# Opening two output tiles at once in the first chunk of an attention-plus-MLP kernel, with narrower filler matmuls in its prologue

## The chip, the cores and the metric

The kernel runs on one core of one Trainium2 chip. The metric is the device time of one execution in microseconds (us). A core has a matrix engine (TensorE, PE in the profile; PEld is its weight load), a vector engine (VectorE, DVE), a scalar engine (ScalarE, ACT), GpSimd (POOL) and a queue engine (SyncE, SP), each with its own queue of instructions, and 16 DMA engines that they share.

## The reference

```python
B, H, S, D = 8, 8, 576, 64            # q, k, v; s is (B, H, S)
scores = q @ k.T / sqrt(D)
cum = cumsum(maximum(s, 0), -1)
bias = -(cum[..., :, None] - cum[..., None, :])
scores = where(causal, -1e9, scores + minimum(bias, 0))
attn = softmax(scores) @ v            # per batch and head
x = attn as (B * S, H * D)            # 4608 tokens x 512
h = x @ w_in                          # 512 -> 2048
out = gelu_exact(h) @ w_out           # 2048 -> 512
```

## The kernel before

The tokens are worked on in nine chunks of 512 (NCH = 9), the attention in eight batches of eight heads, taken as four pairs of heads (p = 0 to 3). The order of all work is written out by hand; each engine runs its instructions in the order of the program, and the framework adds the waits. While the MLP of chunk c runs, the attention of batch c + 1 is placed between its pieces.

The pieces, with their lines:

- `tr_item(b, p, i)` (353) transposes one pair's q (i = 0) or k (i = 1) on PE with 18 small matmuls, and a copy, mostly on DVE (364), puts the result into `qkT`. Only batches 0 and 1 are transposed so.
- `sc_item(b, p)` (370) makes the scores of a pair in two units, u = 0 and 1 (376), in two-bank tiles. ACT takes the exponential into P (392), and DVE applies the causal mask (401, 406). In the prologue the mask is partly added on PE (384).
- `av_item(b, p)` (452) multiplies P with v and with the weights (414), and `norm` (427) divides by way of a logarithm and an exponential on ACT (431, 432) and a product on DVE (447), which fills `xT`, the input of the MLP. `av_rest` and `norm_rest` do the last 64 tokens of a batch.
- `l1_item(c, f2)` (482) is the MLP's first layer, for two blocks of 128 columns of w_in (495), with the Gelu on ACT (501, 504) into `gT`.
- `l2_item(c, sub, f0, f1, av)` (506) is the second layer for 128 tokens: one output tile `o_ps` of 128 x 512 is the sum of 16 matmuls (514), ft = 0 to 15; f0 and f1 say which of the 16 this call issues. The call that ends at 16 also issues the copy of the tile on DVE (521) and the output's DMA on SP (523). ft = 0 to 7 read the first half of w_out, 8 to 15 the second.
- `scale_pair(b, p)` (550) scales one pair's part of v on DVE (230).
- `keep_busy(n)` (559) issues n filler matmuls of 512 columns on a zero tile, into `warm`; nothing reads it.

On-chip accumulation memory (PSUM) has eight banks of 128 x 512 fp32. Four are the two "sc" tiles (scores, first layer, wide attention outputs), three are "av" (transposes, attention outputs, some output tiles), one is "mlp" (an output tile, or `warm`). With `av=False` an output tile takes the "mlp" bank, with `av=True` one of the three "av" banks. A tile takes its bank at its first matmul and gives it back after its last reader.

Loads go through POOL's queue in the order of the program: q and k of batch 0, v of batch 0, w_in in four parts (`load_w(0, i)`), then the first halves of q and k of batch 1, w_out in four parts (`load_w(1, i)`), the second halves of q and k, v of batch 1, and q and k of batch 2.

The change touches the prologue, from line 563 on, in which filler matmuls stand between the transposes and scores of batch 0, and the branch `c == 0` of the loop over chunks, lines 630 to 676. There, once chunk 0's first layer is done, its four output tiles (sub = 0 to 3) are computed between the transposes, scores and attention outputs of batch 1.

Of the kernel before, what the change touches and what calls it, by code (L numbers as in the profile page):

```python
# [19 lines left out]
def kernel(  # L20
# [10 lines left out]
    nc = tc.nc  # L31
# [92 lines left out]
    busy = const.tile([128, 512], bf16, name="busy")  # L124
# [245 lines left out]
    def sc_item(b, p, neg=False, masks=True):  # L370
        P_of[b, p] = P = work.tile([128, 2, PW], bf16, tag="P", bufs=4, name="P")
        for u in range(NU):
            s_ps = ps.tile([128, 2, 512], fp32, tag="sc", bufs=2, name="sc_ps")
            for jt, i0, n, off in UNITS[u]:
                for e in range(2):
                    nc.tensor.matmul(  # L376
                        s_ps[:, e, off : off + n],
                        lhsT=qkT[b % 2][e * 64 : e * 64 + 64, 1, p, jt * 128 : jt * 128 + 128],
                        rhs=qkT[b % 2][e * 64 : e * 64 + 64, 0, p, i0 : i0 + n],
                        start=True, stop=not neg, skip_group_check=neg,  # L380
                    )
            for lo, n, w in ((0, 2, 128), (448, 1, 64))[: u + 1 if neg else 0]:
                for e in range(2):
                    nc.tensor.matmul(  # L384
                        s_ps[:, e, 0:512].rearrange("p (g c) -> p g c", c=256)[:, :, 0:128]
                        if n == 2 else s_ps[:, e, lo : lo + w],
                        lhsT=ident_bf,
                        rhs=neg_bf[:, :w].unsqueeze(1).to_broadcast([128, n, w])
                        if n == 2 else neg_bf[:, :w],
                        start=False, stop=True, skip_group_check=True,  # L390
                    )
            nc.scalar.activation(  # L392
                P[:, :, UO[u] : UO[u] + UW[u]], s_ps[:, :, : UW[u]], func=AF.Exp, scale=scale
            )
            if masks and not neg:
                mask_item(b, p, u, nc.vector)
# [109 lines left out]
    def l2_item(c, sub, f0=0, f1=FT, av=False):  # L506

        gT = gT_of[c]
        if f0 == 0:
            tag, bufs = ("av", 3) if av else ("mlp", 1)  # L510
            o_of[c, sub] = ps.tile([128, KO * 128], fp32, tag=tag, bufs=bufs, name="o_ps")
        o_ps = o_of[c, sub]
        for ft in range(f0, f1):
            nc.tensor.matmul(  # L514
                o_ps, lhsT=gT[:, ft, sub * 128 : (sub + 1) * 128], rhs=w_out_r[:, ft, :],
                start=(ft == 0), stop=(ft == FT - 1),
            )
        if f1 < FT:
            return
        o_sb = work.tile([128, KO * 128], fp32, tag="osb", bufs=3, name="o_sb")  # L520
        nc.vector.tensor_copy(o_sb, o_ps)  # L521
        r0 = c * NB + sub * 128
        nc.sync.dma_start(out=out[r0 : r0 + 128, :], in_=o_sb)
# [32 lines left out]
    load_v(0, (ST - 1,))  # L556
    warm = ps.tile([128, 512], fp32, tag="mlp", bufs=1, name="warm")

    def keep_busy(n):
        for _ in range(n):  # L560
            nc.tensor.matmul(warm, lhsT=busy[:, :128], rhs=busy, start=True, stop=True)

    weights_scan()
    keep_busy(8)
    tr_item(0, 0, 0, nc.scalar.copy)
    tr_item(0, 0, 1)
    weights_dve()
    keep_busy(3)
    sc_item(0, 0, masks=False)
    tr_item(0, 1, 0)  # L570
    keep_busy(1)
    tr_item(0, 1, 1)
    nc.vector.tensor_scalar(neg_bf, tri_bf, 2048.0, -2048.0, op0=MULT, op1=ALU.add)
    weights_pe()
# [31 lines left out]
    for c in range(NCH):  # L606
        nb = c + 1
        for k0, k1 in ((0, 2), (2, 3)) if c == 0 else ((0, 3),):
            l1_item(c, 0, k0, k1)
            l1_item(c, 1, k0, k1)  # L610
        l1_item(c, 0, KO - 1)
        l1_item(c, 1, KO - 1)
        l1_item(c, 2, av=True)
        if 0 < c and nb < B:
            scale_v(nb, STS, nc.vector)
            absmax_v(nb)
        if c == 0:
            absmax_v(0)
            scale_v(0, STS[ST - 1 :], nc.vector)
        if c < B:  # L620
            for p in range(NP):
                absmax(c, p)
        if 1 < c and nb + 1 < B:
            nc.gpsimd.tensor_copy(pace, gT_of[c][:, 0, 0:1])
            load_v(nb + 1)
            if nb + 2 < B:
                load_qk(nb + 2)
        for f2 in range(3, FT // 2):
            l1_item(c, f2)
        if c == 0:  # L630
            exp_set()
            load_v(2)
            for p in range(NP):
                av_rest(0, p)
            tr_item(1, 0, 0)
            tr_item(1, 0, 1)
            l2_item(c, 0, 0, 8)
            tr_item(1, 1, 0)
            tr_item(1, 1, 1)
            norm_rest(0)  # L640
            sc_item(1, 0)
            l2_item(c, 0, 8)
            sc_item(1, 1)
            l2_item(c, 1, 0, 8, av=True)
            tr_item(1, 2, 0)
            tr_item(1, 2, 1)
            l2_item(c, 1, 8, av=True)
            tr_item(1, 3, 0)
            tr_item(1, 3, 1)
            scale_pair(1, 0)  # L650
            sc_item(1, 2)
            l2_item(c, 2, 0, 8)
            scale_pair(1, 1)
            sc_item(1, 3)
            l2_item(c, 2, 8)
            scale_pair(1, 2)
            av_item(1, 0, rest=False)
            scale_pair(1, 3)
            av_item(1, 1, wide=True, rest=False)
            l2_item(c, 3, 0, 8)  # L660
            interleave(2, "q")
            write_rows(2, 0, nc.sync)
            av_item(1, 2, wide=True, rest=False)
            l2_item(c, 3, 8)
            interleave(2, "k")
            write_rows(2, 1, nc.sync)
            av_item(1, 3, rest=False)
            for p in (0, 1):
                transpose_rows(2, p)
            gelu_set()  # L670
            for p in (2, 3):
                transpose_rows(2, p)
            nc.gpsimd.tensor_copy(pace, qkT[0][:, 1, 3, 0:1])
            load_qk(3)
            load_v(3)
            absmax_v(1)
        elif nb < B:
            exp_set()
            l2_item(c, 0, 0, 4)
            if c == 1:  # L680
                for p in range(NP):
                    av_rest(1, p)
            sc_item(nb, 0)
            if c == 1:
                norm_rest(1)
            l2_item(c, 0, 4)
            late = int(c == 1)
            for p in range(1, NP):
                if nb + 1 < B and p == 1 + late:
                    interleave(nb + 1, "q")  # L690
                    write_rows(nb + 1, 0, nc.sync)
                if nb + 1 < B and p > 1 and not late:
                    transpose_rows(nb + 1, p - 2)
                sc_item(nb, p)
                av_item(nb, p - 1)
                l2_item(c, p, 0, 12)
                if p == NP - 1:
                    if nb + 1 < B:
                        for pt in range(0 if late else p - 1, NP):
                            transpose_rows(nb + 1, pt)  # L700
                    if c == 1:
                        nc.gpsimd.tensor_copy(pace, qkT[(nb + 1) % 2][:, 1, p, 0:1])
                        load_qk(nb + 2)
                    av_item(nb, p)
                    norm_rest(nb)
                    gelu_set()
                l2_item(c, p, 12)
                if nb == B - 1 and p == 1:
                    cert_decay()
                if nb + 1 < B and p == 1 + late:  # L710
                    interleave(nb + 1, "k")
                    write_rows(nb + 1, 1, nc.sync)
        else:
            if c == B - 1:
                cert_1()
            for sub in range(4):
                if c == NCH - 1 and sub == 3:
                    l2_last(c, sub)
                    break
                l2_item(c, sub, av=sub % 2 == 0)  # L720
                if c == B - 1 and sub < 3:
                    (cert_2, cert_3, cert_4)[sub]()
# [4 lines left out]
    with tc.If(rv > 0):  # L727
        with tc.tile_pool(name="gen", bufs=1) as gen, tc.tile_pool(
# [21 lines left out]
            with tc.For_i(0, B, 1) as b:  # L750
# [8 lines left out]
                for h in range(H):  # L759
# [17 lines left out]
                    for it in range(ST):  # L777
                        n_i = 128 if it < ST - 1 else SL
                        w = min(S, (it + 1) * 128)
                        s_ps = gps.tile([128, 1024], fp32, tag="g2", bufs=2, name="gs_ps")  # L780
                        for j0 in range(0, w, 512):
# [3 lines left out]
                                rhs=tT["k"][:, j0:j1], start=True, stop=True,  # L785
# [20 lines left out]
                        for jt in range(it + 1):  # L806
# [9 lines left out]
                                lhsT=raw["v"][:n_j, jt, h0 : h0 + 2, :].rearrange("p h d -> p (h d)"),  # L816
                                rhs=pT[:n_j, :n_i], start=(jt == 0), stop=(jt == it),
# [5 lines left out]
            with tc.For_i(0, NCH, 1) as c:  # L823
                g = gen.tile([128, FT, NB], bf16, name="gg")
                for ft in range(FT):
                    h_ps = gps.tile([128, NB], fp32, tag="g4", bufs=1, name="gh_ps")
                    for ko in range(KO):
                        nc.tensor.matmul(
                            h_ps, lhsT=w_in_r[:, ko, ft * 128 : (ft + 1) * 128],
# [44 lines left out]
```

## Time and profile before

| | us |
|---|---|
| median of six runs | 331.74 |
| lowest and highest of the six | 330.57 and 333.61 |
| the profiled execution | 332.1 |
| its span, first to last instruction | 330.2 |
| PE busy in the span | 317.6 |
| ACT busy | 203.1 |
| DVE busy | 192.8 |
| POOL busy | 65.4 |
| start of the steady first layer of chunk 0 (495) | 23.09 |
| first output tile's first matmul | 38.13 |

The profile is of one execution, and times in it count from its first instruction. A timeline row gives the start, the duration, the engine, the line, the operation, the tile written and those read, the shapes, how many instructions are merged in the row, and in brackets how long the engine stood idle before it and what ended that. A matmul's duration in such a row includes the time in which it drains; starts of successive matmuls tell what one costs. A few matmul records are missing from the trace, so a count can be one short.

### The profile page before, as it was taken

What the parts mean: (1) busy time and instruction counts of PE and PEld (TensorE: products, weight loads), DVE (VectorE), ACT (ScalarE), POOL (GpSimd) and SP (SyncE); (2) the same over time, 40 slices, a digit from 0 to 9 for tenths busy, and PEclk for the clock granted to TensorE, in tenths of its full rate; (3) what the DMA queues carried; (4) which work ended last, traced back from release to release, by engine and by line L of the source; (5) the groups of instructions that cost most, each with busy time, mean ns of one, the idle gap of its engine ahead of it and who ended that gap; (6) DMA issues with size and microseconds to landing.
All of it is one profiled execution on the core that took longest, in us unless ns stands there. A gap on an engine that the chain in (4) does not pass through costs nothing.

```text
span 330.2 us, 6357 instructions
## 1 busy us (share of the span) xinstructions
PE 317.6 (96%) x2540; PEld 164.2 (50%) x2585; DVE 192.8 (58%) x384; ACT 203.1 (62%) x288; POOL 65.4 (20%) x100
## 2 busy tenths in 40 slices
PE   6989999999999999999999999999999999999992
PEld 2654555445554555445544554455445544444452
DVE  5749378896569364946395748755783664150021
ACT  4697657759566857677577757677659566204400
POOL 8753243005300730610043003200000000000000
PEclk9699999999999999999999999999999999999998
DMA  7999999855985899999669665527500110010012
GB/s 116 221 210 204 206 185 241 284 93 88 242 266 107 149 250 275 208 131 232 218 133 232 177 177 126 138 105 172 137 3 34 52 48 0 34 64 32 3 64 71
DMA packets 53828, 47.30 MB, mean 143 GB/s; under 512 B 31328, under 2 KB 43872, under 8 KB 53792
## 3 DMA queue, kind: packets, MB, share of 16 engines
q0 software_dynamic: 15936, 23.07, 39.7%
q1 hardware_dynamic: 37856, 23.75, 26.3%
q8 instruction: 22, 0.36, 0.5%
q14 instruction: 14, 0.11, 0.1%
HBM read 36.85 MB, written 16.52 MB: 162 GB/s over the span
## 4 chain that ended last, share of the span: by engine, by line
PE 92%; DMA 2%; DVE 1%; issue 1%; ACT 1%; POOL 1%; POOLq 0%
PE h_ps L495 37%; PE o_ps L514 37%; PE sc_ps L376 5%; PE avn L414 4%; PE avd L414 3%; DMA early_k<-in_k_dram 2%; PE avr L414 1%; PE tr_ps L359 1%; PE o_ps L533 1%; PE avw L414 1%; PE sc_ps L384 0%; DVE qkT L364 0%; POOL early_q L115 0%; ACT ln L432 0%; ACT ln L431 0%
## 5 line engine op out<-in xcount | busy, mean ns | idle before, releaser
L514 PE MATMUL o_ps<-w_out_r,gT 128*128 128x512 bf16 x533 | 127.3, 380 | 1.7 <-issue 0.5
L495 PE MATMUL h_ps<-xT,w_in_r 128*128 128x512 bf16 x560 | 125.2, 379 | 1.5 <-DVE xT L447 0.6
L495 PEld LDWEIGHTS <-w_in_r 128*128 128x128 bf16 x576 | 56.2, 98 | 68.6 <-issue 1.1
L501 ACT ACTIVATE gT<-h_ps 128x1024 bf16<-128x1024 f32 x54 | 54.3, 1022 | 49.4 <-PE h_ps L495 49.4
L392 ACT ACTIVATE P<-sc_ps 128x1024 bf16<-128x1024 f32 x64 | 62.2, 1021 | 33.5 <-PE sc_ps L376 31.1
L514 PEld LDWEIGHTS <-gT 128*128 128x128 bf16 x560 | 51.6, 98 | 59.0
L521 DVE COPY o_sb<-o_ps 128x512 f32<-128x512 f32 x35 | 24.1, 687 | 46.4 <-PE o_ps L514 46.4
L401 DVE TENSOR_TENSOR P<-P,tri_bf 128x512 bf16<-128x512 bf16 x58 | 23.9, 422 | 36.8 <-ACT P L392 36.4
L213 DVE TENSOR_REDUCE amx<-qkT 128x2 f32<-128x1152 bf16 x32 | 40.9, 1336 | 0.0
L447 DVE SCALAR_TENSOR_TENSOR xT<-avn,ln 128x256 bf16<-128x256 f32 (+3 forms) x64 | 21.7, 386 | 24.9 <-ACT ln L432 24.8
L202 POOL DMA_DIRECT2D raw_v<-in_v_dram x40 | 34.2, 880 | 9.9 <-DMA w_out_r<-in_moe_w_out_dram 4.1
L431 ACT ACTIVATE ln<-avd 128x256 f32<-128x256 f32 x56 | 18.6, 392 | 12.4 <-PE avd L414 11.0
L230 DVE TENSOR_TENSOR vv<-raw_v,wb 128x512 bf16<-128x512 f32 (+3 forms) x44 | 25.2, 634 | 0.8 <-DMA raw_v<-in_v_dram 0.8
L432 ACT ACTIVATE ln<-ln 128x512 f32<-128x512 f32 (+1 forms) x40 | 23.5, 587 | 1.3
L504 ACT ACTIVATE gT<-h_ps 128x512 bf16<-128x512 f32 x36 | 19.6, 603 | 6.3 <-PE h_ps L495 6.3
L220 DVE TENSOR_REDUCE amv<-raw_v 128x1 f32<-128x2048 f32 (+1 forms) x16 | 23.0, 1471 | 0.0
L376 PE MATMUL sc_ps<-qkT 64*128 64x256 bf16 (+2 forms) x320 | 21.9, 258 | 0.5 <-DVE vv L230 0.4
L376 PEld LDWEIGHTS <-qkT 64*128 64x128 bf16 x320 | 13.2, 96 | 14.8 <-issue 12.4
L414 PEld LDWEIGHTS <-vv 128*64 128x64 bf16 x384 | 16.9, 109 | 6.9 <-issue 4.1
L414 PEld LDWEIGHTS <-wb 128*64 128x64 bf16 x384 | 17.1, 111 | 0.0
L414 PE MATMUL avn<-P,vv 128*64 128x256 bf16 x224 | 16.1, 265 | 0.0
L414 PE MATMUL avd<-P,wb 128*64 128x256 bf16 x224 | 15.4, 259 | 0.0
(94 smaller groups left out, 158.5 us busy)
## 6 DMA issues: line engine op xcount, KB each, us to landing
out_dram<-o_sb SPq DMA_DIRECT2D x35, 256.0 KB, 2.3
raw_v<-in_v_dram POOLq DMA_DIRECT2D x32, 256.0 KB, 8.0
rows<-qk_bf SPq DMA_DIRECT2D x12, 576.0 KB, 6.1
early_q<-in_q_dram POOLq DMA_DIRECT2D x14, 288.0 KB, 10.7
early_k<-in_k_dram POOLq DMA_DIRECT2D x14, 288.0 KB, 11.4
w_in_r<-in_moe_w_in_dram POOLq DMA_DIRECT2D x4, 512.0 KB, 11.1
w_out_r<-in_moe_w_out_dram POOLq DMA_DIRECT2D x4, 512.0 KB, 15.7
raw_v<-in_v_dram POOLq DMA_DIRECT2D x8, 128.0 KB, 9.7
```

What stands on the lines that cost most here:

```text
L202: nc.gpsimd.dma_start(out=t[:n_st, st, :, :], in_=bass.AP(tensor=v.tensor, offset=v.offset + b * H * S * D + st * 128 * D, ap=[[D, n_st], ...
L213: nc.vector.tensor_reduce(amx[:, b * NP + p], qkT[b % 2][:, :, p, :S], axis=AX, op=ALU.max, apply_absolute_value=True)
L230: eng.tensor_tensor(vb[:n_st, st0:st1, h0:h1, :], t[:n_st, st0:st1, h0:h1, :], wb[:n_st, st0:st1, b * H + h0 : b * H + h1] .unsqueeze(3).t ...
L376: nc.tensor.matmul(s_ps[:, e, off : off + n], lhsT=qkT[b % 2][e * 64 : e * 64 + 64, 1, p, jt * 128 : jt * 128 + 128], rhs=qkT[b % 2][e * 6 ...
L392: nc.scalar.activation(P[:, :, UO[u] : UO[u] + UW[u]], s_ps[:, :, : UW[u]], func=AF.Exp, scale=scale)
L401: eng.tensor_tensor(d, d, tri_bf.unsqueeze(1).unsqueeze(1).to_broadcast([128, 2, 2, 128]), op=MULT)
L414: nc.tensor.matmul(out[e * 64 : e * 64 + 64, lo : lo + n], lhsT=(wb[:, jt, b * H + h : b * H + h + 1].to_broadcast([128, 64]) if den else ...
L432: nc.scalar.activation(ln[:, :w], ln[:, :w], func=AF.Exp, scale=-1.0)
L495: nc.tensor.matmul(h_of[c, f2][i], lhsT=w_in_r[:, ko, ft * 128 : (ft + 1) * 128], rhs=xT[:, ko, c * NB % XW : c * NB % XW + NB], start=(ko ...
L501: nc.scalar.activation(gT_of[c][:, f2 * 2 : f2 * 2 + 2, :], hh_of[c, f2], func=AF.Gelu)
L514: nc.tensor.matmul(o_ps, lhsT=gT[:, ft, sub * 128 : (sub + 1) * 128], rhs=w_out_r[:, ft, :], start=(ft == 0), stop=(ft == FT - 1),)
L521: nc.vector.tensor_copy(o_sb, o_ps)
```

## The change

In the prologue `keep_busy` gets a width: the three fillers ahead of the first scores and the one ahead of the second pair's k become 256 columns wide in place of 512. The eight at the start and the one ahead of the last scores stay at 512.

In chunk 0 the first half of the second output tile (sub = 1) is issued ahead of the second half of the first (sub = 0), so that both are open at once, the first in the "mlp" bank and the second in an "av" bank. The third tile (sub = 2) goes into an "av" bank in place of the "mlp" bank.

```diff
-    def keep_busy(n):
+    def keep_busy(n, w=512):
         for _ in range(n):
-            nc.tensor.matmul(warm, lhsT=busy[:, :128], rhs=busy, start=True, stop=True)
+            nc.tensor.matmul(warm[:, :w], lhsT=busy[:, :128], rhs=busy[:, :w], start=True, stop=True)
...
     weights_dve()
-    keep_busy(3)
+    keep_busy(3, 256)
     sc_item(0, 0, masks=False)
     tr_item(0, 1, 0)
-    keep_busy(1)
+    keep_busy(1, 256)
     tr_item(0, 1, 1)
...
             sc_item(1, 0)
+            l2_item(c, 1, 0, 8, av=True)
+            sc_item(1, 1)
             l2_item(c, 0, 8)
-            sc_item(1, 1)
-            l2_item(c, 1, 0, 8, av=True)
             tr_item(1, 2, 0)
             tr_item(1, 2, 1)
             l2_item(c, 1, 8, av=True)
...
             sc_item(1, 2)
-            l2_item(c, 2, 0, 8)
+            l2_item(c, 2, 0, 8, av=True)
             scale_pair(1, 1)
             sc_item(1, 3)
-            l2_item(c, 2, 8)
+            l2_item(c, 2, 8, av=True)
```

## The prediction

> **What bounds the kernel now.** I read the page first: busy time by engine, then the slices.
>
> ```profile
> span 330.2 us, 6357 instructions
> PE 317.6 (96%) x2540; PEld 164.2 (50%) x2585; DVE 192.8 (58%) x384; ACT 203.1 (62%) x288; POOL 65.4 (20%) x100
> PEclk9699999999999999999999999999999999999998
> ```
>
> TensorE (PE) is busy for 96% of the span. The change touches two stretches, the prologue (to 23 us) and the second half of chunk 0 (41 to 55 us). The clock row shows one dent, in the second slice. The windows view, cut at the edges of that dent and one step before and after it, columns PE, PEld, DVE, ACT, POOL busy, then granted clock, DMA share and GB/s:
>
> ```profile
> 4.16:7.57 3.41, 2.69 (x51) 1.34 (x49) 2.69 (x4) 1.03 (x2) 3.41 (x7) 1.00 1.07 147
> 7.57:10.98 3.41, 2.41 (x65) 1.76 (x66) 2.19 (x4) 2.03 (x4) 3.41 (x5) 1.00 1.12 217
> 10.98:14.40 3.42, 3.42 (x70) 2.45 (x70) 1.64 (x5) 2.69 (x3) 3.03 (x6) 0.50 1.04 225
> 14.40:17.81 3.41, 3.05 (x22) 1.28 (x25) 3.37 (x8) 2.20 (x3) 0.52 (x4) 0.50 1.20 204
> 17.81:21.22 3.41, 3.12 (x60) 2.87 (x58) 0.14 (x1) 3.25 (x7) 2.38 (x5) 1.00 1.25 209
> ```
>
> PE runs at half clock from 10.98 to 17.81 us, after two stretches in which it was busy 2.69 and 2.41 of 3.41 us; and DMA is saturated throughout. Then the timelines of the stretch of chunk 0: PE first, then VectorE (DVE), then the POOL queue, which issues the loads.
>
> ```profile
> 40.65 0.61 PE L376 MATMUL sc_ps<-qkT 64*128 64x256 bf16 x10
> 41.20 1.90 PE L514 MATMUL o_ps<-w_out_r,gT 128*128 128x512 bf16 x7
> 43.03 0.61 PE L376 MATMUL sc_ps<-qkT 64*128 64x256 bf16 x10
> 43.57 1.90 PE L514 MATMUL o_ps<-w_out_r,gT 128*128 128x512 bf16 x8
> ```
>
> ```profile
> 40.48 1.42 DVE L364 COPY qkT<-tr_ps 128x576 bf16<-128x576 bf16 x2 [1.10 <-PE tr_ps L359]
> ...
> 43.53 0.68 DVE L521 COPY o_sb<-o_ps 128x512 f32<-128x512 f32 x1
> ...
> 45.92 1.42 DVE L364 COPY qkT<-tr_ps 128x576 bf16<-128x576 bf16 x2
> 48.03 0.69 DVE L521 COPY o_sb<-o_ps 128x512 f32<-128x512 f32 x1 [0.69 <-PE o_ps L514]
> ```
>
> ```profile
> 42.24 0.63 POOL L101 DMA_DIRECT2D early_q<-in_q_dram  x1 [2.92 <-DMA w_out_r<-in_moe_w_out_dram]
> ...
> 45.49 0.61 POOL L101 DMA_DIRECT2D early_q<-in_q_dram  x1 [0.66 <-DMA early_k<-in_k_dram]
> ```
>
> The reader is to see that no PE row names a wait: from 36.8 to 60.5 us PE is busy 23.16 of 23.64 us, and what is missing is the step from one kind of matmul to the next. The bound there is PE's own work. The two POOL rows show how near the loads are: POOL stood on the last quarter of w_out until just before 42.24, and on the second half of batch 1's k until just before 45.49. By the tile view the one was issued at 24.14 and took 17.8 us, landing at 41.96; the other was issued at 27.91 and took 17.3, landing at 45.20.
>
> **What the Trainium skill says.** "TensorE: Matmul & The Clock Gate", section "What's actually happening": the clock is set to half or full by how busy PE was in free-running windows of 3413 ns. The trace agrees in length: the half-clock stretch is 6.83 us, two such windows. The threshold isn't given, and the trace shows only that 2.69 and 2.41 us were together too little. Same page, "Architectural detail": VectorE is a strict FIFO; the trace agrees, no DVE row starts before the one ahead of it. "PSUM — Partial Sum Buffer", "PSUM bank collisions raise a hardware error": order accesses by bank. So a tile in a reused bank waits for the last reader of that bank; two open tiles in two banks do not disturb each other.
>
> **The change, part by part.** No instruction is added or removed, apart from the width of four fillers.
>
> (1) *Fillers.* Four of 512 columns become 256. Three starts at full clock lie 0.216 to 0.225 us apart (timeline at 5.82, 6.05 and 6.26 us), so half the width removes about 0.11 us each, 0.43 us in all, of PE work. None of it is on the path: the three end near 6.5 to 6.6, and the scores behind them start at 6.75, when DVE's copy into qkT (5.93 + 0.76 = 6.69) is done. The fourth starts at about 8.75 and ends before 9.03, when the transposes behind it start on k from DMA (idle before them 0.30, released by early_k). Direct worth: 0.0. Cover gone: had the loads come earlier, at most 0.11 + 0.32 us. The indirect cost is that the first stretch above falls from 2.69 to about 2.37 us busy, and the second from 2.41 to 2.30. If the clock then drops one window sooner (7.57), PE's work from 9.03 to 10.98, continuous, is done at half speed: 0.98 us lost. If it also returns one window later (21.22), another 3.12 / 2 = 1.56. A gain is bounded below in the rivals. Value taken: 0, since the dent came without the change and the same dent stays likeliest.
>
> (2) *Second tile's first half ahead of the first tile's second half.* Both are eight matmuls of 0.216 us (1.83 us with the step), so PE's order is shifted by nothing: scores at 43.03, transposes at 45.40 as before. What moves is the needs. The last quarter of w_out, landed at 41.96, was read at 41.20 + 4 x 0.216 = 42.07, a margin of 0.11 us; now it is read at 43.57 + 0.86 = 44.44, a margin of 2.5. In this execution that removes no wait. The next load behind it is k at 45.20, read at 45.71: margin 0.5. So where PE arrives earlier, the gain is the difference of these margins, at most 0.4 us, before k stops it.
> The second tile now takes its bank at 41.20. The three banks of the attention outputs are handed out in the order they came free (the program's addresses of before), so it gets that of the first transpose of pair 1, whose copy starts at 40.48 and takes 0.75: free at 41.23, plus the 0.05 that lies between qkT's copy and the scores at 6.75. Cost: at most 0.1 us, all on PE. Were it the bank of the batch's leftovers (DVE 41.81 + 0.42 = 42.23), it would cost 1.1; that is the upper end, against which the address order speaks.
>
> (3) *DVE's queue.* The first tile's copy (0.68) and its output DMA on SP's queue move from 43.53 to behind the masks of the second scores, which end at 45.99. Queued behind it: the two transposes' copies, 45.92 to 47.34, now 46.67 to about 48.09, and the second tile's copy behind these, from 48.03 to about 48.1. PE's next transposes at 47.92 and 48.23 reuse those two banks, free at about 47.4 and 48.1: margins 0.5 and 0.1. The scores at 48.61 need the second copy: margin 0.5. Cost 0, and 0.1 to 0.2 if DVE runs late. The pieces of v behind it wait for DMA until 50.82 in any case; that hides the shift. SP holds nothing else until 58.69, so the output DMA delays nothing.
>
> (4) *Third tile in an attention bank.* It starts at 49.15 in the bank that the second tile's copy leaves at about 48.8: margin 0.35, cost 0. The first attention pair at 53.36 takes the two others, empty since 50.1. The fourth tile at 55.02 no longer waits for the third's copy (54.05 + 0.68 = 54.73): a margin of 0.29 becomes several us, worth nothing while it was not late.
>
> **Sum.** For the profiled execution, span 330.2 and 332.1 us with what lies around it: 0 (fillers) + 0.1 (bank) + 0 + 0 = 332.2. In executions whose PE is earlier, up to -0.4. That one execution lies 0.4 above the median of the six runs, 331.74, which themselves go from 330.57 to 333.61. I carry the difference over, between +0.1 and -0.4, as about 0: **331.7**.
>
> **Rivals.** *Slower, through the clock.* The thinner fillers leave the window from 4.16 to 7.57 under the threshold. For it: PE's 2.69 us there is already close to the 2.41 after which the clock fell, and 0.32 goes away. Against it: fillers at 1.20 to 4.55 are unchanged, and the fall came a whole window after the idle gap, so two windows may count. Price: 0.98 for one window, 2.54 for two, thus 332.7 to 334.3; it passes 0.5% (1.66 us) from the point where the clock also comes back later. I name 334.0. Chance 0.2.
> *Faster, through the clock and the loads.* If the dent starts a window earlier and ends one earlier, 14.40 to 17.81 is run at full clock: 3.05 / 2 = 1.5 gained, 0.98 lost. But k at 45.20 caps what arrives, at 0.5 us in this execution; over 0.5% needs the loads earlier as well, which tracing may well delay. Time 330.0. Chance 0.1.
> *It doesn't do what it says*, two tiles opened together relieve no wait, since PE showed none: this is the forecast itself, with the small signs above. Chance 0.7.
>
> **How the numbers follow.** The 0.7 has its own range, 330.6 to 332.8: -0.4 to +0.2, plus the scatter of a median drawn from runs that lie 3.0 us apart, about 0.8 either way. The range for 8 in 10 reaches into the slower rival for one window, and a little to the faster: 330.2 to 333.4. About 0.5% is what a measurement of this kernel can tell from no change. Faster by more: 0.09; within: 0.71; slower by more: 0.20, the two-window case and a late bank together.
>
> **What would show it.** Right: the o_ps rows at about 41.3 and 43.6 with transposes at 45.4 or 45.5; no wait on w_out or on DVE above 0.1 us; the clock dent still two windows of 3.41 us. Step 1 is wrong if the dent begins one window earlier or lasts three. Step 2 is wrong if PE stands over 0.1 us ahead of the second tile on DVE, or if w_out had held PE in the runs that were not traced. Step 3 is wrong if transposes or scores after 47.9 us wait on DVE's copies. A median outside 330.2 to 333.4 would say that an effect in the prologue, and not the order of the tiles, decides.

## The result and the profile after

The changed kernel takes 333.05 us (median; 329.81 to 334.92) against 331.62 for the kernel before in the same comparison: ratio **1.0030**, 95% interval 1.0015 to 1.0044. It is slower by about 1.0 us. The medians lie 1.4 us apart, since the times fall into groups and a median jumps between them; the means, 332.88 and 331.88, differ by 1.00, as the ratio does. Executions that were disturbed as a whole are left out of the ratios, the means and the counts below. The time lies in the predicted range, 330.2 to 333.4, and within the 0.5% that the text calls no change, but the forecast said 331.7 and none, and the interval excludes none.

The profiled execution took 332.84 us. First the head of its page (busy time by engine, then the granted clock in 40 slices):

```profile
span 331.1 us, 6358 instructions
PE 318.9 (96%) x2541; PEld 165.0 (50%) x2585; DVE 193.3 (58%) x384; ACT 203.1 (61%) x288; POOL 65.5 (20%) x100
PEclk9589999999999999999999999999999999999998
```

The dent in the clock is deeper. The windows view of the same execution, cut at its own changes of clock (columns as before: PE, PEld, DVE, ACT, POOL busy, clock, DMA share, GB/s):

```profile
5.05:8.46 3.41, 2.16 (x64) 1.54 (x60) 1.93 (x3) 1.20 (x2) 3.41 (x6) 1.00 1.11 163
8.46:11.87 3.41, 3.41 (x52) 2.07 (x52) 2.38 (x4) 1.86 (x4) 3.41 (x6) 0.50 1.15 245
11.87:15.29 3.42, 3.42 (x70) 2.39 (x69) 1.60 (x5) 2.69 (x3) 2.64 (x6) 0.50 1.06 209
15.29:18.70 3.41, 3.05 (x24) 1.31 (x23) 3.24 (x7) 2.33 (x3) 0.18 (x1) 0.50 1.24 207
18.70:22.11 3.41, 3.18 (x62) 2.93 (x58) 0.27 (x1) 3.25 (x7) 3.39 (x5) 1.00 1.24 208
```

Here the clock fell at the end of the first window at full clock, in which PE was busy 2.16 us, and stayed at half for three windows, 10.24 us; before it had fallen after the second and stayed for two. Chunk 0's first layer starts its unbroken run at 23.85 us in place of 23.09.

The stretch of chunk 0, PE, then DVE:

```profile
41.41 0.61 PE L376 MATMUL sc_ps<-qkT 64*128 64x256 bf16 x10
42.05 1.89 PE L514 MATMUL o_ps<-w_out_r,gT 128*128 128x512 bf16 x7
43.87 0.61 PE L376 MATMUL sc_ps<-qkT 64*128 64x256 bf16 x10
44.41 1.90 PE L514 MATMUL o_ps<-w_out_r,gT 128*128 128x512 bf16 x8
```

```profile
41.24 1.42 DVE L364 COPY qkT<-tr_ps 128x576 bf16<-128x576 bf16 x2 [1.10 <-PE tr_ps L359]
...
46.75 0.69 DVE L521 COPY o_sb<-o_ps 128x512 f32<-128x512 f32 x1
47.35 1.41 DVE L364 COPY qkT<-tr_ps 128x576 bf16<-128x576 bf16 x2
...
48.87 0.69 DVE L521 COPY o_sb<-o_ps 128x512 f32<-128x512 f32 x1
```

From the scores to the second tile it is now 0.64 us (41.41 to 42.05), where the same step took 0.55: that is the 0.1 us of the bank. The first tile's copy has moved behind the masks. Nothing else in this stretch got longer. Of the 0.83 us between the two spans (331.06 and 330.23), 0.76 are there when the first layer starts and 0.09 come here.

### The profile page after: what moved, and what is told of

Same layout as the page of the kernel before. It is cut to its first block, busy times and chain, and to the rows that moved or that the text cites. A ratio compares the mean times of both kernels' runs of the same rounds, so it can differ in the third digit from the quotient of the medians.

```text
span 331.1 us, 6358 instructions
## 1 busy us (share of the span) xinstructions
PE 318.9 (96%) x2541; PEld 165.0 (50%) x2585; DVE 193.3 (58%) x384; ACT 203.1 (61%) x288; POOL 65.5 (20%) x100
## 4 chain that ended last, share of the span: by engine, by line
PE 93%; DVE 2%; DMA 1%; issue 1%; ACT 1%; POOL 0%; POOLq 0%
PE h_ps L495 37%; PE o_ps L514 37%; PE sc_ps L376 6%; PE avn L414 4%; PE avd L414 3%; PE tr_ps L359 2%; PE avr L414 1%; DMA early_k<-in_k_dram 1%; PE o_ps L533 1%; PE avw L414 1%; DVE qkT L364 1%; PE sc_ps L384 1%; ACT ln L432 0%; ACT ln L431 0%; DVE vv L230 0%
## 5 line engine op out<-in xcount | busy, mean ns | idle before, releaser
L364 DVE COPY qkT<-tr_ps 128x576 bf16<-128x576 bf16 x14 | 10.2, 754 | 9.5 <-PE tr_ps L359 9.5
```

## The experiments

Beside the ratio, two counts tell a kernel here: timed executions with a mean clock of 0.980 to 0.988, which means that a half-clock stretch lies inside the prologue, as it does in all six traces with such a mean and in none of the other ten ("dented"), and the others at 333.1 us or more ("upper group"). Each kernel stands beside the runs of before from its own comparison.

| kernel | median, us | before, us | ratio, 95% interval | dented | upper group |
|---|---|---|---|---|---|
| before, in the first four experiments' runs | 331.67 | | | 0 of 67 | 12 of 67 |
| the change | 333.05 | 331.62 | 1.0030 (1.0015 to 1.0044) | 7 of 31 | 15 of 31 |
| e1, thin fillers only | 333.05 | 331.67 | 1.0029 (1.0012 to 1.0047) | 5 of 22 | 9 of 22 |
| e2, order only | 331.73 | 331.67 | 0.9998 (0.9972 to 1.0024) | 0 of 13 | 3 of 13 |
| e3, no such fillers | 332.43 | 331.67 | 1.0017 (0.9998 to 1.0036) | 14 of 21 | 1 of 21 |
| e4, wide ones split | 332.30 | 331.67 | 1.0023 (1.0001 to 1.0045) | 0 of 22 | 7 of 22 |
| e5, twice as many | 332.17 | 332.01 | 0.9993 (0.9972 to 1.0015) | 0 of 22 | 6 of 22 |
| e6, thin, the rest in the gap | 332.48 | 332.01 | 1.0013 (0.9991 to 1.0034) | 0 of 22, and one at 0.974 | 8 of 22 |
| e9, no start fillers | 333.69 | 331.99 | 1.0029 (1.0008 to 1.0051) | 0 of 19 | 13 of 19 |
| e10, more fillers, new order | 331.57 | 331.99 | 0.9984 (0.9964 to 1.0004) | 0 of 22 | 2 of 22 |
| e11, more fillers, old order | 331.93 | 331.99 | 0.9991 (0.9968 to 1.0014) | 0 of 14 | 2 of 14 |

The kernel before had 12 of 68 in the upper group beside the change, 14 of 43 beside e5 and e6, and 15 of 51 beside e9 to e11. In the comparisons of the experiments it has 41 of 161 in the upper group and none dented. Of the 41, 11 have a mean clock of 0.990 to 0.992 and 30 one of 0.995 to 0.999; none of the former kind was traced.

**e1 and e2, one part alone.** Theory A is the clock: thin fillers let it fall. Theory B is the order: the bank and DVE's queue.

```diff
# e1
-    keep_busy(3)
+    keep_busy(3, 256)
...
-    keep_busy(1)
+    keep_busy(1, 256)
     tr_item(0, 1, 1)
```

> Only the four fillers are half as wide; the order of the tiles is that of before. Theory A (the clock: with thinner fillers TensorE falls to half clock in a window sooner, or stays there longer, in more executions): this part alone carries the whole loss, ratio to before 1.003, median about 332.6 to 333.0, and single runs lie in two groups some 1.5 to 2 us apart, with more of them in the upper one than before (12 of 68 above 332.9 before, 17 of 32 after). Theory B (the order of the tiles: bank wait and the vector engine's queue): no change, ratio 0.999 to 1.001.

```diff
# e2
             sc_item(1, 0)
+            l2_item(c, 1, 0, 8, av=True)
+            sc_item(1, 1)
             l2_item(c, 0, 8)
-            sc_item(1, 1)
-            l2_item(c, 1, 0, 8, av=True)
...
-            l2_item(c, 2, 0, 8)
+            l2_item(c, 2, 0, 8, av=True)
...
-            l2_item(c, 2, 8)
+            l2_item(c, 2, 8, av=True)
```

> Only the order and the banks of chunk 0's output tiles are changed; fillers are as wide as before. Theory A: ratio 0.999 to 1.001, with a stall of 0.1 us at most ahead of the second tile in the trace. Theory B: the whole loss is here, ratio 1.003, and the trace shows TensorE idle for about 1 us in all between 41 and 61 us beyond what the kernel before shows there.

The fillers alone give the whole loss, 1.0029, and the order none that shows, 0.9998, with an interval that ends at 1.0024, short of 1.003. Theory B falls. The windows view of e1's trace, columns as above:

```profile
4.18:7.59 3.41, 1.84 (x45) 1.08 (x45) 2.46 (x4) 0.74 (x2) 3.41 (x7) 1.00 1.06 151
7.59:11.01 3.42, 3.42 (x69) 2.59 (x66) 2.16 (x4) 2.28 (x4) 3.42 (x6) 0.50 1.17 223
```

This execution has nearly the phase of the traced one of before (changes at 4.18 and 4.16 us). There 2.69 us of PE in the first window kept the clock; here 1.84 did not, and the half-clock stretch again lasted 10.24 us. The loads moved as well: the first k landed 0.7 us later than before, which alone idles PE, so the fillers do not account for all 0.85 us.

**e3 and e4, taking the fillers away and splitting them.**

```diff
# e3
-    keep_busy(3)
...
-    keep_busy(1)
     tr_item(0, 1, 1)
```

> The four fillers are left out altogether, order of before. Theory A: worse than half width, ratio 1.003 to 1.008, since the busy share of the window falls by as much again; the dent in the clock begins at or before the first window after the loads arrive in every traced execution. Theory B: no change or a little faster, 0.999 to 1.001, since fillers only stand in the way.

```diff
# e4
-    keep_busy(3)
+    keep_busy(6, 256)
...
-    keep_busy(1)
+    keep_busy(2, 256)
     tr_item(0, 1, 1)
```

> Each of the four wide fillers is split into two half as wide, so that the columns stay the same and only the count doubles; order of before. Theory A in its form of busy time: no change against before, ratio 0.999 to 1.001. If it is the width of a single filler, and not their sum, that counts for the clock (more weight loads and gaps), it comes out slower, like the narrow fillers, 1.003.

Without fillers two executions in three are dented (14 of 21), as theory A says, but the ratio is smaller than expected. The traced execution, 330.96 us with a mean clock of 0.986, has a stretch of two windows (9.04 to 15.87 us) in place of three; it is the fastest of all of e3, and the other 13 dented ones have means of 0.981 to 0.984, near those of the traces with three windows (0.980 to 0.983), so it doesn't explain the ratio. What e3 lacks is the upper group, 1 of 21; why, was not traced. e4 missed its expectation: 1.0023, though no run was dented. Its interval nearly reaches 1, and its upper group, 7 of 22 against 12 of 67, isn't clearly larger. Whether splitting costs anything stays open.

**e5 and e6, giving busy time back.**

```diff
# e5
-    keep_busy(3)
+    keep_busy(6)
...
-    keep_busy(1)
+    keep_busy(2)
     tr_item(0, 1, 1)
```

> Order of before, but six and two wide fillers where there were three and one: 0.86 us of TensorE more at full clock. If the clock is kept by the busy sum in a window: no run with a mean clock of 0.98 to 0.987 (a half-clock stretch in the middle of the prologue), as in before and unlike the thin fillers (5 of 22), and fewer runs above 332.9 than the thin fillers' 12 of 22; against it the direct delay of the first scores, some 0.5 us at full clock and 1.3 at half, of which the wait for loads hides a part: ratio 0.998 to 1.003. If the clock plays no role and fillers only cost what they take, the ratio is 1.001 to 1.003 and the spread of the single runs is that of before.

```diff
# e6, on top of e1
     sc_item(0, 0, masks=False)
+    keep_busy(2)
     tr_item(0, 1, 0)
```

> The fillers are thin as in the change, and the 0.43 us taken from them are given back as two wide fillers behind the first scores, where TensorE stands idle for the loads of the second pair; order of before. If the busy sum in a window decides: back to before, ratio 0.999 to 1.001, and hardly a run with a mean clock below 0.988. If it is the place (that TensorE is busy right behind the first transposes) it stays at the thin fillers' 1.003.

Neither has a run between 0.980 and 0.988, and e5 is level with before. e6 returns the columns taken away to another place, behind the first scores; the dents go but for one execution, at 0.974 and 334.35 us, which has more half clock than any dented one (against 5 of 22 for e1). That their place doesn't count is likely from this, not shown. Its ratio, 1.0013, lies between before and the thin fillers, and its interval holds both 1 and 1.003; its upper group, 8 of 22, is no larger a share than the 14 of 43 of before beside it.

**e7, e8 and e12 to e14, the thin fillers in further phases.** e7, e8, e12 and e13 are the kernel of e1, e14 is the changed kernel.

> The kernel with thin fillers only, traced again to catch another phase of the windows in which the clock is set. Theory of the clock: if this execution takes 333.2 us or more with a mean clock of 0.998 or 0.999, the first record of full clock comes only after 14 us, so that the prologue ran at half clock from the start; if it takes 332.3 to 333.1 at 0.98, the half-clock stretch is three windows, 10.2 us; if it takes under 331.9, there is no half-clock stretch after the fillers.

> As the run before it: the same kernel once more, for another phase. An execution at 333.2 us or more with a mean clock of 0.998 or 0.999 shows full clock only after 14 us; one at 0.98 a half-clock stretch of 10.2 us; one under 331.9 none.

> Thin fillers only, a further phase. By the traces so far the clock falls at the end of a window at full clock in which TensorE was busy 2.56 us or less of 3.41, and stays where it was busy 2.62 or more: this trace should keep to that. An execution at 333.2 us or more with a mean clock of 0.998 or 0.999 shows its first full clock only after 14 us.

> Thin fillers only, order of before, one execution. If it takes 333.2 us or more with a mean clock of 0.998 or 0.999, the first record of full clock comes after 14 us; any other execution leaves this open. In either case a window at full clock with TensorE busy below 2.5 us ends in half clock.

> The changed kernel itself, one more execution, with the same question: at 333.2 us or more and a mean clock of 0.998 or 0.999 the first full clock comes after 14 us; at 0.98 a half-clock stretch of about 10.2 us behind a window busy less than 2.6 us.

e7 (332.34 us), e8 (330.38) and e12 (332.51) came as written. The first window at full clock after the start fillers, in this order; a fence for each kernel:

```profile
4.87:8.28 3.41, 2.56 (x68) 1.68 (x66) 2.38 (x4) 1.87 (x3) 3.41 (x6) 1.00 1.10 154
8.28:11.70 3.42, 3.41 (x53) 2.20 (x53) 2.61 (x4) 1.45 (x4) 3.42 (x5) 0.50 1.16 235
```

```profile
5.09:8.50 3.41, 2.81 (x82) 1.92 (x76) 2.44 (x4) 1.94 (x3) 3.41 (x6) 1.00 1.07 156
8.50:11.92 3.42, 3.32 (x99) 2.39 (x93) 2.34 (x5) 2.78 (x5) 3.42 (x6) 1.00 1.14 246
11.92:15.33 3.41, 2.62 (x30) 1.54 (x32) 2.91 (x8) 3.19 (x5) 2.62 (x6) 1.00 1.06 210
```

```profile
5.19:8.60 3.41, 2.45 (x72) 1.71 (x68) 2.30 (x4) 1.55 (x2) 3.41 (x7) 1.00 1.13 163
```

At 2.56 and 2.45 us busy the clock fell at the window's end and stayed at half for 10.24 us; at 2.81, 3.32 and 2.62 it stayed full. In e8 the fillers were just as thin; its loads came so that PE had little to wait for, and it is the shortest traced execution of all, span 328.6 us.

e13 and e14 caught the upper group: 333.60 and 333.46 us. Their mean clock is 0.994, not 0.998, since more of the idle end of the program lies in half clock; but the first record of full clock comes at 20.57 and 20.62 us. Ahead of its first record the windows view shows 1.00, so the durations have to be read. PE's timeline of e14:

```profile
4.72 0.69 PE L359 MATMUL tr_ps<-ident_bf,early_q 64*64 64x64 bf16 x18
5.41 0.69 PE L359 MATMUL tr_ps<-ident_bf,early_k 64*64 64x64 bf16 x18
6.03 0.82 PE L561 MATMUL warm<-busy 128*128 128x256 bf16 x3
...
19.63 0.96 PE L414 MATMUL avw<-P,vv 128*64 128x256 bf16 x8
20.38 0.67 PE L414 MATMUL avw<-P,wb 128*64 128x256 bf16 x8
20.88 0.55 PE L414 MATMUL avw<-P,vv 128*64 128x256 bf16 x8
```

Eight matmuls of one shape take 0.96 us ahead of 20.6 and 0.55 behind it, and 18 transposes 0.69, as in the half-clock stretch of the other traces (0.47 at full clock). This prologue ran at half clock from its start. Going back in steps of 3.413 us from 20.62, its windows met at 0.14, 3.55, 6.97 and 10.38 us, so that the start fillers, 1.20 to 4.8 us without a break, were cut in two: 2.35 us of them lay ahead of 3.55. In the trace of before the window that ended in full clock, 0.74 to 4.16, held 2.96 us of them. A later window of e14, at half clock (the 1.00 is that of a clock not yet on record):

```profile
6.97:10.38 3.41, 3.41 (x59) 2.50 (x61) 1.89 (x4) 2.01 (x3) 3.41 (x4) 1.00 1.07 162
```

PE is busy throughout, and the clock did not come, nor after the next two like it.

**e9, a prologue that is always late to full clock.**

```diff
# e9
     weights_scan()
-    keep_busy(8)
     tr_item(0, 0, 0, nc.scalar.copy)
```

> The kernel before without the eight fillers at its start; the later ones stay wide. TensorE then stands idle until the first q has landed (4.4 to 4.8 us), so by the theory of the clock it gets full clock late in every execution, and most runs lie in the upper group, 333.2 to 334.0 us, with a mean clock of 0.995 to 0.999 and the first record of full clock after 9 us in the trace: ratio 1.004 to 1.006. If the upper group has another cause than a prologue at half clock, the ratio is 0.999 to 1.001 and the groups stay as they were.

13 of 19 runs are in the upper group, and the traced execution (334.2 us) has its first full clock at 20.97 us. A prologue at half clock thus takes the upper group's time, though not every execution of that group need be one (e11 below). The ratio, 1.0029, is a little under the expectation; 5 of 19 still took 332.22 us or less.

**e10 and e11, more fillers where PE waits, with the new and the old order.**

```diff
# e10 (on top of e2) and e11 (on top of before)
     sc_item(0, 0, masks=False)
+    keep_busy(3)
     tr_item(0, 1, 0)
```

> Wide fillers as before, three more wide ones behind the first scores (where TensorE waits for loads), and the change's order and banks of chunk 0's tiles. Theory of the clock: no run with a mean clock of 0.98 to 0.988, fewer in the upper group than before; with the new order the last quarter of w_out is not waited for: ratio 0.996 to 0.999. If fillers behind the scores stand in the way of the second pair's transposes, 1.000 to 1.002.

> The same three more wide fillers behind the first scores, with the order of before. Beside the run with the new order it tells what that order is worth once the clock is kept: by the margins of the prediction (the last quarter of w_out read 2.4 us later, the next load 0.5 us behind it) this kernel is 0.1 to 0.5 us slower than that one, ratio to before 0.997 to 1.000, and a trace with the first layer starting before 22 us shows TensorE waiting for w_out at 39 to 42 us. If the order is worth nothing, both give the same.

e10 lies below the change clearly, 0.9984 against 1.0030 with intervals that do not meet, each against before in its own comparison, and below before perhaps: its interval reaches 1.0004. Its upper group is the smallest but one, 2 of 22. e11 is 0.0007 above it, some 0.2 us, in the expected direction and not resolved. What the order does when PE is early can be read in traces. PE in the old order, e8:

```profile
40.53 1.02 PE L514 MATMUL o_ps<-w_out_r,gT 128*128 128x512 bf16 x4 [0.83 <-DMA w_out_r<-in_moe_w_out_dram]
```

and in the new order, e2 and then e10:

```profile
44.84 0.47 PE L359 MATMUL tr_ps<-ident_bf,early_k 64*64 64x64 bf16 x18 [0.54 <-DMA early_k<-in_k_dram]
```

```profile
44.25 0.47 PE L359 MATMUL tr_ps<-ident_bf,early_k 64*64 64x64 bf16 x18 [0.17 <-DVE P L406]
```

The old order makes an early PE wait for the last quarter of w_out (also 1.31 us in e4's trace and 1.77 in e5's). The new one doesn't; it waits for k instead, or for DVE. e5 in the old order and e2 in the new start the first layer at the same time, 21.43 and 21.44 us. e5 waits its 1.77 us for w_out and starts chunk 1's first layer at 60.72 us, e2 at 59.61: up to there the order is worth 1.1 us in this pair. e2 doesn't keep it, as it loses 1.2 us later on (below), and both spans are 330.6 us. e10's trace has also the one window that breaks the pattern above:

```profile
12.17:15.58 3.41, 2.52 (x46) 1.45 (x41) 2.86 (x7) 3.20 (x5) 2.34 (x6) 1.00 1.08 213
15.58:18.99 3.41, 3.19 (x54) 2.63 (x55) 2.00 (x5) 2.88 (x5) 0.00 (x0) 1.00 1.24 208
```

2.52 us busy, and the clock stayed. So PE's busy time in a window tells nearly, not exactly, what the clock does.

e11's own trace, 333.49 us, belongs to the upper group and starts its first layer at 22.59 us, too late to show a wait for w_out. It is no prologue like e14's. Full clock came at 9.39 us, behind this window:

```profile
5.98:9.39 3.41, 3.08 (x32) 1.55 (x32) 1.37 (x2) 1.00 (x2) 3.41 (x6) 1.00 1.06 152
```

e6's trace, 332.25 us, has it at 9.94 us. Both have wide fillers behind the first scores, where e13 and e14 have none and stay at half until 20.6; that such fillers shorten a prologue at half clock is what four traces suggest, and no more. What e11 loses, it loses later. DVE and then PE, near 90 us:

```profile
88.31 0.83 DVE L178 COPY qk_bf<-early_q 128x1152 bf16<-128x1152 bf16 x2 [3.61 <-DMA early_q<-in_q_dram]
```

```profile
90.72 0.57 PE L414 MATMUL avd<-P,wb 128*64 128x256 bf16 x8 [0.51 <-DVE xT L447]
```

DVE stands on a load of q, its masks and products come late, and PE waits for them; the same returns near 120 us. From chunk 1's first layer at 60.14 us to chunk 3's at 131.42 this execution takes 71.28 us, the changed kernel's 69.57 (61.30 to 130.87). e2 and e6 lose 1.2 and 0.8 us there. e5 and e2 show what it does to a gain made ahead of it. So the scatter of the times has a second source, which lies behind the prologue; the traces of the change, e1, e7, e12, e13 and e14 take 69.6 us for this stretch and show no such wait.

## Why the prediction was wrong

**Step 1 failed**, the fillers: "Value taken: 0, since the dent came without the change and the same dent stays likeliest." Two things were wrong in it.

First, the dent in the shown profile was the exception. None of the 161 timed runs of before is dented; the profiled execution was. What stood for the usual case was one phase of a free-running window. The usual execution of before is not dented. Thin fillers bring a dent into a quarter of the runs (7 of 31), and more of them fall into the upper group (15 of 31, against 12 of 68 before), of which both traced with thin fillers ran at half clock from the start. That the loss is in the fillers is shown (e1, e2). That the clock carries it is shown in the traces of both kinds (dented: the change, e1, e7, e12; half clock from the start: e13, e14), and the counts agree; that every further execution in the upper group is of the latter kind is not shown. An estimate from the times, against the mean of 331.48 us that before takes outside its upper group: the 7 dented ones (mean 332.70) carry 7/31 x 1.22 = 0.28 us, the upper group (15 at 333.57, less 12 of 68 at 333.75 before) 0.61, the other nine 0.11.

Second, the rival was priced rightly and weighted wrongly. It gave 0.98 us for a clock that falls one window sooner; the traced execution after has that, counted from its first window at full clock, and starts the first layer 0.76 us later than the dented one of before. That the price is also near the whole loss of 1.0 us is luck, since dents carry about 0.3 of it. The profile held the argument against my weight: in its own trace 2.69 us in a window kept the clock and 2.41 lost it, and my own sum put the first window of the thin fillers at 2.37, under the loser. I set this aside with the thought that two windows might count. The runs show that one is enough (2.56, 2.45, 2.16 and 1.84 us, each in the first full window). A loss through the clock should have been the forecast.

The other kind of loss, the larger by that estimate, was not among my cases at all: that full clock may not come until 20.6 us, when an edge cuts the start fillers in two. It has no place in the sum. Why thinner fillers, which come behind the start, make such executions more frequent stays open: no trace of before caught that phase.

**Step 2 held in its sum.** The bank cost 0.09 us, estimated at most 0.1. One of its own signs of being wrong did come: in the old order w_out holds an early PE in executions other than the profiled one (e4, e5, e8). That k stops the relief is seen in e2, where PE waits 0.54 us for it. The cap of 0.4 us was too low: in the pair e5 and e2 the order is worth 1.1 us up to chunk 1, for k landed about 2 us behind w_out in e2 (POOL waits for w_out until 42.80, PE for k until 44.84), and 3.2 in the trace that the cap was read from. Over the whole program the order's net is nothing that these runs can tell: 0.9998.

**Step 3 held.** The first tile's copy came at 46.75 and the transposes' copies at 47.35, which is the forecast (45.99 and 46.67) plus the 0.76 by which this execution was behind, within 0.1. No PE instruction waited for them.

**Step 4 held**: no wait shows at the third or the fourth tile.

**The carrying over** of the profiled execution to the median, "as about 0", failed with step 1, because that execution was no typical one. The Trainium skill, "TensorE: Matmul & The Clock Gate", "What's actually happening", says that the windows run freely and don't start with the kernel; the phases of the traces here (first full clock at 4.16, 5.05 and 20.62 us) agree. I had cited the windows' length and not drawn from it that one trace shows one phase only.

## What to carry to other kernels

A filler matmul whose own time is hidden is not free to remove: what it does for the clock in its 3.41 us window can be worth more than its own 0.1 us: the four here, 0.43 us of PE work shorter, made the kernel 1.0 us slower. Where a clock is set by windows that run freely, price an edit over the phases, and count in the timed runs (mean clock and time) whether the profiled execution is a usual one. Where PE waits for loads, more wide ones cost nothing that these runs could tell (e5, e11). Narrower ones where PE is busy anyway were not tried. And a gain in one stretch can be lost at a later load: compare spans, not only the start of the next stage.

## What the runs showed of the hardware

- Eight fillers without a break, 1.20 to 4.8 us, did not bring full clock where an edge near 3.5 us cut them (e13, e14: 2.30 and 2.35 us of PE ahead of it); with 2.96 us ahead of an edge at 4.16 they did (before). Three later windows of e14, 6.97 to 17.21 us, in which PE was busy 3.41 of 3.41 us at half clock, mostly with small transposes and scores, did not bring it either; one of e11 with 3.08 us did. So PE's busy time in a window does not by itself tell whether full clock comes. What counts (rows, columns, or the idle time within a row) stays open.
- Once full, the clock fell after windows with 1.84 to 2.56 us of PE busy and stayed, in every trace up to 25 us, after those with 2.62 or more; one with 2.52 stayed.
- The half-clock stretch came out in whole windows: 6.83 us in two traces (before, e3), 10.24 in four (the change, e1, e7, e12).
